# A fence between row tiles, read by two engines: sliding-window attention and a SwiGLU block on one core

## The chip, the core and the metric

The kernel runs on one core of a Trainium2 chip. A core has a matrix engine (TensorE, PE in the profile, with its weight loads on a row of their own, PEld), a vector engine (VectorE, DVE), a scalar engine (ScalarE, ACT), GpSimd (POOL) and SyncE (SP). Each engine has its own queue of instructions and works through it in order; between engines only semaphores order the work. PE writes its results to PSUM, a memory of eight banks of 128 partitions x 512 float32 values, from which DVE and ACT read them.

The metric is the time of one execution on the device in microseconds (us). Before the change it is 323.75 us, the median of 3 runs (323.66 to 324.06).

## The reference

Eight sequences of 576 tokens, 8 heads of 64 values each. Every token attends to itself and the 63 tokens before it. The result goes, as 4608 tokens of 512 values, through a SwiGLU block with 1536 hidden values:

```python
scores = (1 / sqrt(64)) * q @ k.transpose(0, 1, 3, 2)
mask = (rel >= 0) & (rel < 64)              # rel = row - column
attn = softmax(where(mask, scores, -1e9))
x = (attn @ v) laid out as 4608 x 512
g = x @ w_gate                              # 512 x 1536
out = (g * sigmoid(g) * (x @ w_val)) @ w_out    # 1536 x 512
```

## The kernel before

The 4608 tokens are worked on in nine passes of 512 tokens (t = 0 to 8). Passes 0 to 6 and 8 are the first 512 tokens of a sequence each; pass 7 (`LAST`) gathers the last 64 tokens of all eight sequences, so its scores come in 64-column pieces and there are twice as many of them. The order of the instructions is written out by hand, in Python, and each engine keeps to it. A tracking layer adds the semaphores: an instruction waits for the writers and readers of the tiles and PSUM banks that it touches.

All matmuls take bfloat16 operands. The products of the SwiGLU block use the whole 128x128 array of PE. The attention uses quarters of it: a matmul with 64 rows of operands and 64 columns of weights takes one of two **row tiles** (partitions 0 to 63 or 64 to 127 of the operands, `half(0)` and `half(1)`) and one of two column tiles (the upper or lower half of a bank). Matmuls in different quarters run at the same time.

From pass 2 on (`for t in range(1, NT)`, line 759), the attention of pass t is interleaved with the output projection of pass t-1. In the order of the code:

- `set_exp` loads ACT's table for exponentials and logarithms. `scores(t, 0)` (lines 253 to 279) writes the scores of the first four heads into the PSUM tiles `two[0]` and `two[1]`; `weigh` (line 281) makes the exponentials on ACT into `eb` (line 285), and each returned `masked()` multiplies by the mask (line 290) and adds two halves (line 295) on DVE.
- `project_quads(t - 1, tiles, range(12), 0)` (lines 464 to 475) is the first part of the output projection for token groups 0 and 2, in 64x64 quarters: row tile 0 adds up group 0 in bank 5, row tile 1 adds up group 2 in bank 7. Each covers half of the sum, over 12 blocks: 48 matmuls.
- **The fence.** The second part, `project_quads(..., 1)`, swaps the two: row tile 0 goes on with group 2 in bank 7, row tile 1 with group 0 in bank 5. A row tile may not go on in a bank while the other row tile is still writing there. So `marker(b, x)` (line 377), a 64x16 matmul of ones on row tile x into bank b, is put behind the first part on each row tile: row tile 0 into bank 4, row tile 1 into bank 6. DVE reads one value a partition from each bank into the 64x1 tile `seen` (line 768). Behind the scores of the second four heads stands one more marker, on row tile 1 into bank 6 (line 773). It overwrites what DVE reads, so it waits for DVE; and everything behind it on PE waits with it.
- Between the fence's two ends stand `masks[1]()` on DVE and `scores(t, 1)` on PE, with their exponentials on ACT and masks on DVE.
- The second part of the projection runs in two stretches (7 and 5 blocks, 28 and 20 matmuls), with `sums(t, 0, ...)` between them: PE adds up the weights (line 313) and ACT takes the logarithm (`log`, line 327). `mix_half` (line 391) multiplies weights and values, first into `two[1]`, then into `two[0]`, where the sums stood. Then come the sums of the second four heads in banks 4 and 6, the inverses (line 330), the ends of the projection (`project_end`, line 477: a copy out of PSUM by `nc.scalar.copy` or DVE, and DMAs on SP) and the remaining token groups 1 and 3 (line 459).
- `scale_all` (line 407) writes xT, and 12 calls of `gate_value` (line 446) make the gate and value products (line 450), SiLU on ACT (line 443) and their product hT on DVE (line 444), with the turning of the next pass's q and k on DVE in between (lines 208 and 218). POOL issues the loads of the pass after next once xT is there (line 791).

The short names `on_v`, `on_p` and `on_a` (line 574) are copies by DVE, POOL and ACT.

Of the kernel before, what the change touches and what calls it, by code (L numbers as in the profile page):

```python
# [9 lines left out]
FP32 = mybir.dt.float32  # L10
# [7 lines left out]
def kernel(  # L18
# [11 lines left out]
    S, D, H = 576, 64, 8  # L30
# [6 lines left out]
    cst = ctx.enter_context(tc.tile_pool(name="cst", bufs=1))  # L37
# [8 lines left out]
    bank = [two[i][:, j] for i in range(2) for j in range(2)]  # L46
# [13 lines left out]
    tri = cst.tile([P, 2, 64], BF16, name="tri")  # L60
    bias = cst.tile([P, 2, 4, 4, 2, 16], BF16, name="bias")
    seen = cst.tile([D, 1], FP32, name="seen")
    past = cst.tile([P, 1], BF16, name="past")
    mask = cst.tile([P, 8, 2, 16, 4], BF16, name="mask")

# [92 lines left out]
    def load_last_v():  # L158
        for c in range(2):
            for hd in range(H):  # L160
                w, x, h = hd // 4, hd // 2 % 2, hd % 2
                s0 = S - P + 64 * c
                nc.gpsimd.dma_start(
                    vl[64 * x:64 * x + 64, :, c, w, h],
                    v[:, hd, s0:s0 + 64].rearrange("b r d -> r b d"),
                )
# [4 lines left out]
    def stage_v(t):  # L171
        new_v(t)
        load_halves(nc.sync, staged[t, "v"], t)

    def cast_v(t):
        for i in range(4):
            js = slice(2 * i, 2 * i + 2)
            nc.gpsimd.tensor_copy(vb[t % 2][:, js], staged[t, "v"][:, js])
# [71 lines left out]
    def half(x):  # L250
        return slice(64 * x, 64 * x + 64)

    def scores(t, w):

        qT = queries[t]
        s_ps = two[0], two[1]
        for j in range(8):
            if t == LAST:
                k_j = kT[t % 2 if j < 4 else 2]
                pieces = [(j, j + 1, 0, k_j, P * (j % 4) + 64),  # L260
                          (j, j + 1, 1, k_j, P * (j % 4))]
            else:
                pieces = [(j, min(8, j + 2), 0, kT[t % 2], 64 * j)]
            for lo, hi, c, src, k0 in pieces:
                for h in range(2):
                    for x in range(2):
                        slot = s_ps[h][half(x)].rearrange("r a b -> r (a b)")
                        n = hi - lo
                        o = P * j + 64 * c
                        nc.tensor.matmul(  # L270
                            slot[:, o:o + 64 * n].rearrange(
                                "r (n e y) -> r e n y", n=n, e=16
                            ),
                            src[half(h), 2 * w + x, k0:k0 + 64],
                            blocks(qT[half(h), 2 * w + x], t, lo, hi).rearrange(
                                "r e (n y) -> r e n y", n=n
                            ),
                        )
        return [weigh(t, w, h, s_ps[h]) for h in range(2)]
# [20 lines left out]
    def ready(masks):  # L300
        for masked in masks:
            masked()
# [35 lines left out]
    def sums(t, w, tiles):  # L338
        r = room(2)
        totals(t, w, tiles if len(tiles) > 1 else [tiles[0][:, x] for x in range(2)])  # L340
        for x in range(2):
            inverse[t, 2 * w + x] = r[:, x]
        if len(tiles) > 1:
            for x in range(2):
                logs(t, r[:, x:x + 1], tiles[x].rearrange("r (b x) -> r b x", b=1))
        else:
            logs(t, r, tiles[0])
        return lambda: invert(r)
# [28 lines left out]
    def marker(b, x):  # L377
        nc.tensor.matmul(bank[b][0:D, 0:16], ones[half(x), 0:D], ones[half(x), 0:16])  # L378
# [39 lines left out]
    def mix_half(t, w, pair):  # L418
        mix(t, w, (pair[:, 0], pair[:, 1]))

    def scale_all(t, pairs):
        for u in range(4):
            scale(t, u, pairs[u // 2][:, u % 2])
# [32 lines left out]
    def project_part(t, ss, tiles, cs):  # L456
        for c in cs:
            for s, o_ps in zip(ss, tiles):
                nc.tensor.matmul(  # L459
                    o_ps[:], hT[t][:, c, P * s:P * s + P], wo[:, c, :],  # L460
                    start=(c == 0), stop=(c == 11),
                )

    def project_quads(t, tiles, cs, back):

        for c in cs:
            for y in range(2):
                for x in range(2):
                    s = 2 * (x ^ back)
                    r0 = P * s + 64 * y  # L470
                    nc.tensor.matmul(  # L471
                        tiles[s][half(y)], hT[t][half(x), c, r0:r0 + 64],
                        wo[half(x), c, :],
                        start=not back and c == 0, stop=bool(back) and c == 11,
                    )

    def project_end(t, s, o_ps, copy=nc.vector.tensor_copy):
        os_ = fsb.tile([P, 512], FP32, name="os_", tag="os_", bufs=4)
        copy(os_[:], o_ps[:])
        rows = out[S * batch(t):S * batch(t) + 512]  # L480
        if t < TURNED or t == NT - 1:
            if t < TURNED:
                rows = rows.rearrange("(r e) f -> e r f", e=4)[s]
            else:
                rows = rows[P * s:P * s + P]
            if t < TURNED or s == 0:
                for i in range(2):
                    nc.sync.dma_start(rows[half(i)], os_[half(i)])
            else:
                nc.sync.dma_start(rows, os_[:])  # L490
            return
        if t == LAST:
            rows = out.rearrange("(b s) f -> b s f", s=S)[:, 512:S]
            rows = rows.rearrange("b (r e) f -> e b r f", e=16)
        else:
            rows = rows.rearrange("(r e) f -> e r f", e=16)
        for i in range(4):
            nc.sync.dma_start(rows[4 * s + i], os_[32 * i:32 * i + 32])
# [20 lines left out]
    def set_exp():  # L519
        nc.scalar.preload_act_table_set("natural_log_exp_and_others")  # L520

    def set_silu():
        nc.scalar.preload_act_table_set("silu_and_others")
# [50 lines left out]
    on_v, on_p, on_a = nc.vector.tensor_copy, nc.gpsimd.tensor_copy, nc.scalar.copy  # L574
# [184 lines left out]
    for t in range(1, NT):  # L759
        if t > 1:  # L760
            set_exp()
            masks = scores(t, 0)
            masks[0]()
            project_quads(t - 1, tiles, range(12), 0)
            for x in range(2):
                marker(4 + 2 * x, x)
            for x in range(2):
                on_v(seen[:], bank[4 + 2 * x][0:D, 0:1])  # L768
            masks[1]()
            if t == 2:  # L770
                stage_v(3)
            ready(scores(t, 1))
            marker(6, 1)
            project_quads(t - 1, tiles, range(7), 1)
            end = sums(t, 0, two[0:1])
            project_quads(t - 1, tiles, range(7, 12), 1)
            for w in range(2):
                mix_half(t, w, two[1 - w])
            project_end(t - 1, 0, tiles[0], on_a)
            ends = end, sums(t, 1, (bank[4], bank[6]))  # L780
            for end in ends:
                end()
            project_end(t - 1, 2, tiles[2])
            project_part(t - 1, (1,), (bank[5],), range(12))
            scale_all(t, (two[1], two[0]))
            project_end(t - 1, 1, bank[5], on_a)
            project_part(t - 1, (3,), (bank[4],), range(12))
        set_silu()
        if t > 1:
            project_end(t - 1, 3, bank[4], on_v)  # L790
        on_p(past[:], xT[t][:, 3, 0:1])  # L791
        if t + 1 == LAST:
            load_last_v()
        elif t + 1 < NT and t > 1:
            cast_v(t + 1)
        if t + 2 < NT:
            load_qk(t + 2)
            if t > 1 and t + 2 != LAST:
                stage_v(t + 2)
        if t == 2:  # L800
            k_l = cast.tile([P, 4, 4, 4 * D], BF16, name="k_l", tag="c0")
        if t in (2, 3):
            load_k(k_l, [(b, S - P) for b in range(4, 8)], quarters[2 * t - 4:2 * t - 2])
        turns = (6, 7, 9, 10) if t == 1 else (1, 4, 7, 10)
        for m in range(12):
            gate_value(t, m)
            if m in turns and t + 1 < NT:
                turn(t + 1, turns.index(m))
            if (t, m) in late:
                turn_k(kT[2], k_l, late.index((t, m)))  # L810
# [32 lines left out]
```

## Time and profile before

| what | before |
| --- | --- |
| median of 3 runs | 323.75 us (323.66 to 324.06) |
| the profiled execution's own time | 324.43 us |
| its span, first to last instruction | 322.1 us |
| mean granted TensorE clock | 0.999 |
| PE busy | 314.7 us (98%) |
| DVE busy | 210.9 us (65%) |
| ACT busy | 170.0 us (53%) |
| POOL busy | 146.9 us (46%) |
| PE, line 450 (gate and value products), 814 matmuls | 211.2 us |
| PE, line 459 and line 471 (output projection) | 55.7 us and 40.0 us |
| DVE reads of the fence, line 768 | 14 of 150 ns, 2.1 us |

The profile is one execution. The span is inside the execution's own time; 2.3 us lie around it. Busy time of PE counts a matmul from its start to its modelled end, so neighbouring matmuls overlap, and their sum is not work done at full speed. The chain that ended last follows the work back from the last instruction, at each step to what released it. A row of the timeline merges neighbouring instructions of one line: its length is from the first start to the last end, and a bracket tells how long the engine stood idle before it and what ended that.

### The profile page before, as it was taken

The numbers are of one execution on the slowest core, as the hardware profiler recorded it, in microseconds if no ns is written. First come the engines' busy times: TensorE is split into PE (matmuls) and PEld (weight loads), VectorE is DVE, ScalarE is ACT, GpSimd is POOL, SyncE is SP. The second block draws the span as 40 slices with busy tenths as digits, with TensorE's granted clock in tenths as the row PEclk, the third lists the DMA queues.
The fourth block names the chain that finished last, engine by engine and source line by source line (L and its number), as shares of the span: only waits on it lengthen the run. The fifth ranks groups of instructions, "written<-read, shape, count | busy, mean of one in ns | idle before, by whom it ended". The sixth has DMA issues, their size and how long they took to land.

```text
span 322.1 us, 8061 instructions
## 1 busy us (share of the span) xinstructions
PE 314.7 (98%) x3269; PEld 155.4 (48%) x3299; DVE 210.9 (65%) x349; ACT 170.0 (53%) x232; POOL 146.9 (46%) x267
## 2 busy tenths in 40 slices
PE   8999999999999999999999999999999999999996
PEld 4644444445444544455445544454446444544443
DVE  4856756498586846776588656866896476844422
ACT  4963666348633863377336933584347633873310
POOL 4955667867567336740861099507755300000000
PEclk9999999999999999999999999999999999999999
DMA  7999999999699549983896269719998400011003
GB/s 251 202 197 198 207 155 208 201 206 125 141 192 189 57 108 167 196 93 97 146 197 70 65 117 117 76 34 144 185 192 102 101 17 1 4 72 62 0 19 113
DMA packets 83525, 40.42 MB, mean 126 GB/s; under 512 B 64160, under 2 KB 78752, under 8 KB 83488
## 3 DMA queue, kind: packets, MB, share of 16 engines
q0 software_dynamic: 51488, 22.59, 58.1%
q1 hardware_dynamic: 31456, 16.79, 23.1%
q8 instruction: 26, 0.43, 0.5%
q10 hardware_dynamic: 544, 0.52, 0.5%
q14 instruction: 11, 0.09, 0.1%
HBM read 53.02 MB, written 9.44 MB: 194 GB/s over the span
## 4 chain that ended last, share of the span: by engine, by line
PE 95%; DMA 1%; DVE 1%; issue 1%; ACT 1%; DVEq 0%
PE one L450 56%; PE one L459 17%; PE one L471 11%; PE two L391 2%; PE two L270 2%; PE one L426 2%; DMA q_f<-in_q_dram 1%; PE two L313 1%; PE one L512 1%; PE one L196 1%; DVE seen L768 1%; PE two L426 1%; PE one L378 0%; PE one L313 0%; PE two L715 0%
## 5 line engine op out<-in xcount | busy, mean ns | idle before, releaser
L443 ACT ACTIVATE sg<-one 128x512 f32<-128x512 f32 x107 | 63.9, 597 | 118.5 <-PE one L450 90.4
L444 DVE TENSOR_TENSOR hT<-sg,one 128x512 bf16<-128x512 f32 x107 | 74.0, 692 | 62.1 <-PE one L450 58.2
L450 PE MATMUL one<-xT,wv 128*128 128x512 bf16 x408 | 106.4, 379 | 0.9
L450 PE MATMUL one<-xT,wg 128*128 128x512 bf16 x406 | 104.8, 379 | 0.1
L127 POOL DMA_DIRECT2D k_s<-in_k_dram x112 | 60.5, 576 | 25.4 <-DMA q_s<-in_q_dram 12.1
L450 PEld LDWEIGHTS <-wv 128*128 128x128 bf16 x416 | 40.6, 98 | 49.2
L450 PEld LDWEIGHTS <-wg 128*128 128x128 bf16 x416 | 40.5, 98 | 48.9
L459 PE MATMUL one<-wo,hT 128*128 128x512 bf16 x241 | 55.7, 380 | 0.7 <-issue 0.2
L791 POOL COPY past<-xT 128x1 bf16<-128x1 bf16 x8 | 1.5, 190 | 92.0 <-DVE xT L407 92.0
L471 PE MATMUL one<-wo,hT 64*64 64x512 bf16 x672 | 40.0, 377 | 0.0
L459 PEld LDWEIGHTS <-hT 128*128 128x128 bf16 x252 | 23.7, 98 | 29.4 <-issue 2.0
L218 DVE STREAM_TRANSPOSE kT<-k_s 128x512 bf16<-128x512 bf16 x28 | 36.0, 1284 | 0.0
L407 DVE TENSOR_TENSOR xT<-two,r 128x512 bf16<-128x512 f32 x34 | 21.3, 684 | 22.3 <-ACT r L330 18.3
L285 ACT ACTIVATE eb<-two 128x960 bf16<-128x960 f32 (+1 forms) x32 | 29.5, 974 | 6.2 <-PE two L270 6.1
L471 PEld LDWEIGHTS <-hT 64*64 64x64 bf16 x672 | 18.4, 107 | 14.9 <-issue 1.0
L290 DVE TENSOR_TENSOR eb<-eb,mask 128x960 bf16<-128x960 bf16 (+1 forms) x32 | 21.0, 655 | 4.3 <-ACT eb L285 4.2
L208 DVE STREAM_TRANSPOSE qT<-q_s 128x512 bf16<-128x512 bf16 x32 | 22.3, 700 | 0.1
L330 ACT ACTIVATE r<-r 128x1024 f32<-128x1024 f32 (+1 forms) x20 | 18.5, 971 | 0.1
L295 DVE TENSOR_TENSOR both<-eb 128x512 bf16<-128x512 bf16 x32 | 13.6, 425 | 1.1
L92 POOL DMA_DIRECT2D q_s<-in_q_dram x24 | 13.0, 552 | 1.9 <-DMA v<-in_v_dram 1.2
L153 POOL DMA_DIRECT2D vb<-in_v_dram x16 | 10.9, 694 | 6.4 <-DMA wo<-in_moe_w_out_dram 3.7
L520 ACT ACT_TABLE_LOAD x9 | 11.5, 1283 | 2.0 <-issue 1.9
(134 smaller groups left out, 241.0 us busy)
## 6 DMA issues: line engine op xcount, KB each, us to landing
k_s<-in_k_dram POOLq DMA_DIRECT2D x112, 56.0 KB, 5.2
q_s<-in_q_dram POOLq DMA_DIRECT2D x24, 248.0 KB, 6.2
v_f<-in_v_dram SPq DMA_DIRECT2D x40, 128.0 KB
wg<-in_moe_w_gate_dram POOLq DMA_DIRECT2D x5, 256.0 KB, 8.4
wv<-in_moe_w_val_dram POOLq DMA_DIRECT2D x5, 256.0 KB, 9.0
q_f<-in_q_dram SPq DMA_DIRECT2D x4, 256.0 KB
wo<-in_moe_w_out_dram POOLq DMA_DIRECT2D x2, 512.0 KB, 10.7
vb<-in_v_dram POOLq DMA_DIRECT2D x16, 64.0 KB, 6.3
```

The lines of the kernel that those rows point to most:

```text
L127: nc.gpsimd.dma_start(k_s[p0:p0 + 32, g, :, 0:w], k[b, a:H:2, s:s + P].rearrange("u (r e) d -> r u (e d)", e=4) [:, :, 32 * c:32 * c + w],)
L208: nc.vector.transpose(queries[t][:, u, :].rearrange("r (e x) -> r e x", e=16), staged[t][0][:, u].rearrange("r (e d) -> r e d", d=D)[:, :, ...
L218: nc.vector.transpose(dst[:, u, :].rearrange("r (g x e) -> r g e x", g=4, e=4), k_s[:, :, u].rearrange("r g (e d) -> r g e d", d=D)[:, :, ...
L285: nc.scalar.activation(flat, s_ps[:].rearrange("r a b -> r (a b)")[:, 0:n], AF.Exp, scale=0.125)
L290: nc.vector.tensor_mul(flat, flat, mask[:].rearrange("r j c e y -> r (j c e y)")[:, 0:n])
L330: nc.scalar.activation(r, r, AF.Exp, scale=-1.0)
L407: nc.vector.tensor_mul(x, o_ps, r)
L443: nc.scalar.activation(sg[:], g_ps[:], AF.Silu)
L444: nc.vector.tensor_mul(hT[t][:, m, :], sg[:], v_ps[:])
L450: nc.tensor.matmul(ps[:], w[:, c, P * m:P * m + P], xT[t][:, c, :], start=(c == 0), stop=(c == 3),)
L459: nc.tensor.matmul(o_ps[:], hT[t][:, c, P * s:P * s + P], wo[:, c, :], start=(c == 0), stop=(c == 11),)
L471: nc.tensor.matmul(tiles[s][half(y)], hT[t][half(x), c, r0:r0 + 64], wo[half(x), c, :], start=not back and c == 0, stop=bool(back) and c = ...
```

## The change

The fence's two values are read by two engines. ACT reads bank 4 into a new 64x1 tile `fence`; DVE reads bank 6 into `seen`, as before. Behind the second scores there are two markers in place of one: row tile 0 into bank 4, which overwrites what ACT reads, and row tile 1 into bank 6, which overwrites what DVE reads.

```diff
     seen = cst.tile([D, 1], FP32, name="seen")
+    fence = cst.tile([D, 1], FP32, name="fence")
     past = cst.tile([P, 1], BF16, name="past")
...
             project_quads(t - 1, tiles, range(12), 0)
             for x in range(2):
                 marker(4 + 2 * x, x)
-            for x in range(2):
-                on_v(seen[:], bank[4 + 2 * x][0:D, 0:1])
+            on_a(fence[:], bank[4][0:D, 0:1])
+            on_v(seen[:], bank[6][0:D, 0:1])
             masks[1]()
             if t == 2:
                 stage_v(3)
             ready(scores(t, 1))
-            marker(6, 1)
+            for x in range(2):
+                marker(4 + 2 * x, x)
             project_quads(t - 1, tiles, range(7), 1)
```

## The prediction

> **What bounds the kernel now.** I read the profile from the outside in: the engines' busy time, the chain of work that ended last, the timeline around the fence in one token tile (the pass t=2), and the same timeline in the odd pass (t=7). Engine totals and the chain by engine:
>
> ```profile
> span 322.1 us, 8061 instructions
> PE 314.7 (98%) x3269; PEld 155.4 (48%) x3299; DVE 210.9 (65%) x349; ACT 170.0 (53%) x232; POOL 146.9 (46%) x267
> PE 95%; DMA 1%; DVE 1%; issue 1%; ACT 1%; DVEq 0%
> ```
>
> The matrix engine (PE) is busy for 98% of the span and makes up 95% of the chain. So a shorter time can only come from PE work removed or from a place where PE stands still. The other engines matter where PE waits for them. The chain of waits inside the pass t=2, in order of time, shows such a place between two groups of projection matmuls (start, length, what):
>
> ```profile
> 75.02 0.15 DVE seen L768
> 75.17 0.03 issue
> 75.19 0.02 DVEq L768
> 75.21 0.04 issue
> 75.26 0.16 DVE seen L768
> 75.42 0.04 issue
> 75.46 0.17 PE one L378
> ```
>
> The two reads by VectorE (DVE) stand one behind the other in the chain, with 0.09 us of waiting between them, and the marker behind them starts 0.04 us after the second. What the engines do meanwhile, from the timeline of the same stretch (start, length, engine, line, operation, output and input, count):
>
> ```profile
> 71.71 0.62 PE L270 MATMUL two<-qT,kT 64*64 64x128 bf16 x32
> 72.16 2.76 PE L471 MATMUL one<-wo,hT 64*64 64x512 bf16 x48
> 72.86 1.83 ACT L285 ACTIVATE eb<-two 128x960 bf16<-128x960 f32 x2
> 74.56 0.43 DVE L295 TENSOR_TENSOR both<-eb 128x512 bf16<-128x512 bf16 x1
> 74.75 0.17 PE L378 MATMUL one<-ones 64*64 64x16 bf16 x1
> 74.76 0.61 PE L270 MATMUL two<-qT,kT 64*64 64x128 bf16 x31
> 75.00 0.40 DVE L768 COPY seen<-one 64x1 f32<-64x1 f32 x2
> 75.18 0.10 PEld L378 LDWEIGHTS <-ones 64*64 64x64 bf16 x1
> 75.33 0.64 DVE L290 TENSOR_TENSOR eb<-eb,mask 128x960 bf16<-128x960 bf16 x1
> 75.41 1.83 ACT L285 ACTIVATE eb<-two 128x960 bf16<-128x960 f32 x2 [0.72 <-PE two L270]
> 75.46 0.17 PE L378 MATMUL one<-ones 64*64 64x16 bf16 x1
> 75.46 1.22 PEld L471 LDWEIGHTS <-hT 64*64 64x64 bf16 x28 [0.18 <-issue]
> 75.47 1.71 PE L471 MATMUL one<-wo,hT 64*64 64x512 bf16 x28
> ```
>
> The scores of the second head group (L270) cover part of the fence: they end at 74.76+0.61 = 75.37. The ends of matmuls are latencies, though. Without a fence, the first scores end at 71.71+0.62 = 72.33 and the projection starts at 72.16, 0.17 earlier. So the second projection could start at 75.37-0.17 = 75.20, and it starts at 75.47: the fence costs 0.27 us here.
>
> The pass t=7 has twice as many, shorter score matmuls:
>
> ```profile
> 240.49 0.71 PE L270 MATMUL two<-qT,kT 64*64 64x64 bf16 x64
> 241.02 2.77 PE L471 MATMUL one<-wo,hT 64*64 64x512 bf16 x48
> 241.64 1.94 ACT L285 ACTIVATE eb<-two 128x1024 bf16<-128x1024 f32 x2
> 243.61 0.18 PE L378 MATMUL one<-ones 64*64 64x16 bf16 x2
> 243.62 0.77 PE L270 MATMUL two<-qT,kT 64*64 64x64 bf16 x64
> 243.87 0.40 DVE L768 COPY seen<-one 64x1 f32<-64x1 f32 x2
> 244.33 0.17 PE L378 MATMUL one<-ones 64*64 64x16 bf16 x1
> ```
>
> The same arithmetic gives an earliest restart of 243.62+0.77-0.18 = 244.21, with 0.18 = 240.49+0.71-241.02. The restart is at 244.33, so 0.12 us is lost. The fence is in seven passes, t=2 to 8, and the count of its reads says so:
>
> ```profile
> L768 DVE COPY seen<-one x14: 149/150/151, 75.0 to 278.4; 64x1 f32<-64x1 f32 x14
> ```
>
> All fourteen take 149 to 151 ns, so I take six passes like t=2 and one like t=7.
>
> **The change part by part.** Prices for ScalarE (ACT), by shape, and one ACT copy in the same table set:
>
> ```profile
> L285 ACT ACTIVATE eb<-two 128x960 bf16<-128x960 f32 x28 | 25.6, 968 | 5.3 <-PE two L270 5.3
> L285 ACT ACTIVATE eb<-two 128x1024 bf16<-128x1024 f32 x4 | 3.9, 1020 | 0.9 <-PE two L270 0.9
> 78.54 0.59 ACT L479 COPY os__1314<-one 128x512 f32<-128x512 f32 x1
> ```
>
> *One DVE read becomes an ACT read.* No row has a small ACT operation. The two exponentials give (1020-968)/64 = 0.81 ns per element and 968-960x0.81 = 190 ns for none, so a 64x1 copy is put at 0.19 us, an estimate. It cannot sensibly be under the 0.15 us of the DVE read; the upper end is the 128x512 copy, 0.59 us. I take 0.19 because the exponentials, which read the same memory, differ from the copy in length alone. Hops between engines: PE to ACT 0.05 and ACT to PE 0.05, from these rows:
>
> ```profile
> 77.00 0.39 PE L313 MATMUL two<-both,ones 64*64 64x512 bf16 x4
> 77.44 1.02 ACT L327 ACTIVATE r<-two 128x1024 f32<-128x1024 f32 x1 [0.20 <-PE two L313]
> 4.24 0.63 ACT qk_b L577
> 4.92 1.03 PE one L196 x8
> ```
>
> (77.00+0.39 = 77.39 against 77.44; 4.24+0.63 = 4.87 against 4.92.) The first markers end at 74.75+0.17 = 74.92. The ACT read then runs from 74.97 to 75.16 and releases PE at 75.21. ACT is free for it: the exponentials ahead of it end at 72.86+1.83 = 74.69, and in t=7 at 243.58 against markers at 243.79. Behind it on ACT stands the next exponential, which starts at 75.41 when the scores end, 0.25 us after the read is through; if that cover were gone, every us of ACT lateness would be paid by the exponentials.
>
> *The remaining DVE read* starts at 75.00 (its own queue is free at 74.56+0.43 = 74.99) and ends at 75.15; with the 0.04 to 0.06 us from the second read to the marker now, it releases PE at 75.21 too. The DVE work behind it, the mask product at 75.33, moves up by the read and the wait that go, about 0.26 us. PE does not wait for it.
>
> *The own tile for each reader* costs memory of four bytes a row and no instruction. *The second marker* adds one weight load and one 64x16 matmul in each of seven passes. The first markers start within 0.01 us of each other, and the projection's first matmul starts 0.01 us after the marker that waited. So I take 0.02 us a pass. From above, the whole weight load of 0.10 us (L378 at 75.18) could be exposed.
>
> *DMA, POOL and SP:* nothing is added, removed or moved past another; their work starts as much earlier as PE does.
>
> *Sum.* In t=2: released at the latest of 75.21 (ACT), 75.21 (DVE) and 75.20 (PE itself), plus 0.02 for the second marker and the 0.01 that stands today: 75.24 against 75.47, so 0.23 us. Six such passes: 1.38. In t=7 ACT would release at 243.79+0.05+0.19+0.05 = 244.08 and DVE at 243.87+0.15+0.06 = 244.08, both before PE's own 244.21; with the 0.02, 244.23 against 244.33: 0.10. Together 1.5 us. The profiled execution took 324.43 us (its span of 322.1 and 2.3 around it); it becomes 322.9. The median of the runs is 323.75, 0.7 below the profiled one, and becomes **322.3 us**, 0.45% less. A difference of 0.2%, or 0.65 us, is about what measurement can tell.
>
> *A rule on the second marker's weight load.* The row first: the projection's weight load starts at 75.46, with the marker that waited, after 0.18 us in which the loader had nothing issued; so it did not pass the waiting marker. The Trainium skill (TensorE: Matmul & The Clock Gate, The mechanism) says that a weight load for another row group is pulled ahead of matmuls in flight. By that rule the second marker's load, in the other row half, would be hidden and the second marker free, 0.14 us better in all; by the row, it is not pulled past a wait, and up to 0.10 us a pass is exposed. The row decides here, and gives the first rival below.
>
> **The rivals.** *The second marker pays its weight load.* Behind a marker of row tile 0 that still waits stands the load for row tile 1. If it is not hidden, a pass like t=2 loses 0.10 instead of 0.02: 6x0.08 = 0.5 less gain. In t=7 ACT releases 0.13 before PE is done, so it hides. That gives 322.8. For it: the 0.18 us of "issue". Against it: today's projection stands in the same position, and its first matmul is only 0.01 after the marker.
>
> *The gain is given back later in the pass.* The scores stay where they are, so the exponentials do too; only PE behind the fence moves up. Next in line:
>
> ```profile
> 78.30 1.01 PE L391 MATMUL two<-eb,vb 64*64 64x128 bf16 x64
> ```
>
> Its second half writes what the logarithm (L327) reads. That half starts near 78.30+0.4 = 78.70; the logarithm ends at 77.44+1.02 = 78.46. With PE 0.23 earlier the logarithm no longer waits for L313 (77.39 becomes 77.16) but for the exponentials' end at 75.41+1.83 = 77.24; it ends at about 78.30 and is wanted at 78.47. Of 0.24 us slack, 0.17 stay. If I have misplaced a wait by more than that, up to all of the gain goes: 323.75.
>
> *Slower: the ACT read comes late.* The new release decides against the old one when 74.97 + read + 0.05 + 0.02 passes 75.46, at a read of 0.42 us. At 0.59, the upper end, PE restarts 0.17 us later than now in a pass like t=2, and in t=7 at 243.84+0.59+0.05+0.02 = 244.50, 0.17 later too: 7x0.17 = 1.2, so 324.95 us. The DVE reads at 0.15 speak against it, as a read of the same size in the same memory.
>
> *A table load for the copy.* If the copy were not in the loaded set, two loads would stand around each read, 1.28 us each:
>
> ```profile
> L520 ACT ACT_TABLE_LOAD x9 | 11.5, 1283 | 2.0 <-issue 1.9
> ```
>
> Each fence would then release over 1 us later, 7 us and more in all: above 330. Against it: nine loads are one for each of nine token tiles, and the copy at 78.54 runs between a logarithm and the next without one. The Trainium skill (ScalarE: Activation LUTs, Table sets: the hidden batching unit) says that cheap functions such as copy are in every set; the trace agrees.
>
> **How the numbers follow.** Forecast 0.60 (322.3), weight load paid 0.18 (322.8), given back 0.10 (323.75), ACT late 0.11 (324.95), table load 0.01. The first two are faster by over 0.65 us; a few hundredths of the second may fall short of it. So faster 0.76, same 0.12, slower 0.12. The low end is no fence cost at all: 6x0.27+0.12 = 1.7, 322.0, and a little for scatter, 321.9. The high end takes in "given back", 323.8, and leaves out the late read.
>
> **What would show it.** Right: one DVE read of 0.15 us and one ACT read near 0.19 us that start within 0.05 us of each other; the second markers about 0.46 us after the start of the first ones; the projection's second part starting about 0.49 us after them (75.24-74.75) instead of 0.72; no other wait that grows in the seven passes; PE's span 1.5 us shorter with the same busy time. Wrong: an ACT read over 0.4 us, a gap between the second markers near 0.1 us, a wait of L391 for ACT, or a table load beyond nine.

## The result and the profile after

The changed kernel takes 322.15 us (median of 4 runs, 321.89 to 322.59) against 323.9 us of the kernel before (4 runs): a ratio of 0.9946, with a 95% interval of 0.9929 to 0.9963. Measured again later beside 15 runs of the kernel before, it is 0.9929 (0.9916 to 0.9941), 1.9 to 2.7 us less. The forecast was 322.3 us.

The profiled execution of the changed kernel took 321.89 us. Because of the added lines, line 450 is now 451, 471 is 472, and so on; the two reads are lines 768 (ACT) and 769 (DVE). The engine totals and the chain by engine:

```profile
span 319.9 us, 8068 instructions
PE 312.8 (98%) x3276; PEld 154.9 (48%) x3306; DVE 210.1 (66%) x342; ACT 170.9 (53%) x239; POOL 147.0 (46%) x267
PE 96%; DMA 1%; issue 1%; DVE 1%; ACT 1%; DVEq 0%
```

Seven PE instructions more (the second markers), seven DVE instructions fewer and seven more on ACT: that is the edit. The chain of waits in the pass t=2:

```profile
73.98 0.43 PE one L472 x8
74.41 0.46 PE two L271 x30
74.86 0.04 PE one L379 x2
74.90 1.10 PE one L472 x15
```

DVE is gone from it. Where two reads and the waits between them stood, the chain goes from the projection through the scores into the second markers without leaving PE. The chain goes by the modelled ends of matmuls, though: that the fence still costs something is shown below, by the kernel without one. The timeline of the same stretch (start, length, engine, line, operation, output and input, count):

```profile
71.65 2.76 PE L472 MATMUL one<-wo,hT 64*64 64x512 bf16 x48
74.24 0.17 PE L379 MATMUL one<-ones 64*64 64x16 bf16 x1
74.25 0.62 PE L271 MATMUL two<-qT,kT 64*64 64x128 bf16 x31
74.49 0.15 ACT L768 COPY fence<-one 64x1 f32<-64x1 f32 x1 [0.31 <-PE one L379]
74.53 0.15 DVE L769 COPY seen<-one 64x1 f32<-64x1 f32 x1
74.60 0.64 DVE L291 TENSOR_TENSOR eb<-eb,mask 128x960 bf16<-128x960 bf16 x1
74.70 0.20 PE L379 MATMUL one<-ones 64*64 64x16 bf16 x2
74.74 1.27 PE L472 MATMUL one<-wo,hT 64*64 64x512 bf16 x20
74.91 1.83 ACT L286 ACTIVATE eb<-two 128x960 bf16<-128x960 f32 x2 [0.26 <-PE two L271]
```

Both reads take 0.15 us and lie side by side, 0.04 us apart. The second markers go off from 74.70 on, the one into bank 6 at 74.73 (74.70+0.20-0.17), 0.05 us after the DVE read has ended; the projection's second part starts at 74.74. From the first matmul of the first part it is now 74.74-71.65 = 3.09 us, where it was 75.47-72.16 = 3.31 before: 0.22 us less. The pass t=7:

```profile
239.44 2.78 PE L472 MATMUL one<-wo,hT 64*64 64x512 bf16 x48
242.05 0.78 PE L271 MATMUL two<-qT,kT 64*64 64x64 bf16 x64
242.63 0.19 PE L379 MATMUL one<-ones 64*64 64x16 bf16 x2
242.65 1.71 PE L472 MATMUL one<-wo,hT 64*64 64x512 bf16 x28
```

3.21 us here, against 244.33-241.02 = 3.31 before: 0.10 less. I call this time "part 1 to part 2" below. The other stretch, "part 2 to the next part 1", is 30.44 to 30.57 us from t=2 to t=6 in both kernels, so what the fence gives is not taken back by another wait. Behind t=7 it is shorter too, by 0.25 us, which nothing in the change asks for: 275.34-244.33 = 31.01 before, and 30.76 after.

### The profile page after: what moved, and what is told of

Read it like the earlier page. It is cut to its first block, busy times and chain, and to the rows that moved or that the text cites. A ratio compares the mean times of both kernels' runs of the same rounds, so it can differ in the third digit from the quotient of the medians.

```text
span 319.9 us, 8068 instructions
## 1 busy us (share of the span) xinstructions
PE 312.8 (98%) x3276; PEld 154.9 (48%) x3306; DVE 210.1 (66%) x342; ACT 170.9 (53%) x239; POOL 147.0 (46%) x267
## 4 chain that ended last, share of the span: by engine, by line
PE 96%; DMA 1%; issue 1%; DVE 1%; ACT 1%; DVEq 0%
PE one L451 56%; PE one L460 17%; PE one L472 11%; PE two L271 3%; PE two L392 2%; PE one L427 2%; DMA q_f<-in_q_dram 1%; PE two L314 1%; PE one L513 1%; PE two L427 1%; PE one L314 0%; PE one L197 0%; DVE kT L200 0%; PE two L242 0%; PE two L716 0%
```

## The experiments

All times of the table are differences of starts of projection matmuls (lines 471 or 472) in one profile of each kernel; the values of part 1 to part 2 are those of t=2 to 6 and 8, which agree within 0.02 us but for one.

| kernel | part 1 to part 2 | in t=7 | part 2 of t=7 to part 1 of t=8 | first part 1 at | ratio to before (95%) |
| --- | --- | --- | --- | --- | --- |
| before | 3.31 | 3.31 | 31.01 | 72.16 | 1 |
| before, second profile | 3.31 | 3.32 | 31.04 | 71.66 | - |
| before, third profile | 3.31 | 3.31 | 31.25 | 71.66 | - |
| the change | 3.09 | 3.21 | 30.76 | 71.65 | 0.9946 (0.9929 to 0.9963) |
| the change, second profile | 3.09 | 3.21 | 30.76 | 71.64 | 0.9929 (0.9916 to 0.9941) |
| own tiles, both on DVE | 3.12 | 3.19 | 31.35 | 71.89 | 0.9965 (0.9953 to 0.9977) |
| the same with two markers | 3.12 | 3.21 | 30.76 | 71.89 | 0.9952 (0.9939 to 0.9965) |
| own tiles, both on ACT | 3.12 | 3.19 | 30.91 | 72.44 | 0.9963 (0.9949 to 0.9977) |
| before with two markers | 3.31 | 3.31 | 30.79 | 71.65 | 0.9998 (0.9987 to 1.0009) |
| long read on ACT | 3.33 | 3.34 | 30.77 | 72.44 | 0.9994 (0.9984 to 1.0004) |
| no fence | 3.02 | 3.27 | 31.25 | 71.91 | 0.9939 (0.9921 to 0.9956) |
| before, six matmuls more at the start | 3.31 | 3.31 | 30.76 | 71.57 | 0.9989 (0.9977 to 1.0001) |

**Own tiles, both reads on DVE.** The theory was that a second engine gives the gain. Its rival: it is the wait between two writes of one tile.

```diff
-            on_a(fence[:], bank[4][0:D, 0:1])
+            on_v(fence[:], bank[4][0:D, 0:1])
             on_v(seen[:], bank[6][0:D, 0:1])
...
-            for x in range(2):
-                marker(4 + 2 * x, x)
+            marker(6, 1)
             project_quads(t - 1, tiles, range(7), 1)
```

> Both values are read by VectorE, as before, but each into its own tile, and the one marker stays. I look at the time from the first matmul of the projection's first part to the first of its second part: 3.31 us before (72.16 to 75.47 in the pass t=2), 3.09 after the change (71.65 to 74.74). If the gain comes from a second engine, the two reads of 0.15 us still stand in series: they end 0.30 us after the first starts, and the time is 3.20, half of the gain (0.11 x 6 passes and 0.09 in t=7: 0.75 us). If it comes from the wait between two writes of the same tile, the second read can follow the first as closely as the mask product follows a read now (0.07 us, 75.26 to 75.33): reads through 0.22 us after the first starts, the time is 3.12, and nearly all of the gain comes without ScalarE (0.19 x 6 and 0.10: 1.2 us).

Measured: 3.12 us, the number of the rival. The timeline of this kernel, in t=2:

```profile
74.74 0.15 DVE L768 COPY fence<-one 64x1 f32<-64x1 f32 x1
74.82 0.14 DVE L769 COPY seen<-one 64x1 f32<-64x1 f32 x1
75.01 0.17 PE L379 MATMUL one<-ones 64*64 64x16 bf16 x1
75.02 0.63 PE L472 MATMUL one<-wo,hT 64*64 64x512 bf16 x8
```

The reads start 0.08 us apart and overlap; before, they started at 75.00 and 75.26, about 0.25 apart. The row of the kernel before that names the difference is a separate semaphore instruction in DVE's queue (DVEq) at the reads' line, one for each pass:

```profile
L768 DVEq EVENT_SEMAPHORE  x7: 21/21/21, 75.2 to 278.4; - x7
```

The trace has it wait on the very counter that the first read raises at its end; in t=2 it goes off at 75.19, after that end at 75.15. With two tiles it is gone from that line. So the second read waited until the first had written `seen`, and that wait was 0.19 of the 0.22 us. The whole kernel gains less (0.9965) than six times 0.19 and 0.12 make, 1.26 us or 0.9961, by an amount that the interval does not tell apart from nothing; its profile also shows a longer standstill behind t=7, to which I come below.

**Both reads on ACT**, each into its own tile, one marker:

```diff
             on_a(fence[:], bank[4][0:D, 0:1])
-            on_v(seen[:], bank[6][0:D, 0:1])
+            on_a(seen[:], bank[6][0:D, 0:1])
...
-            for x in range(2):
-                marker(4 + 2 * x, x)
+            marker(6, 1)
```

> ScalarE reads both values, each into its own tile, and one marker waits. If what counts is that the reads need not wait for each other, the second read follows the first within about 0.1 us, as on VectorE with own tiles, and the parts stand 3.10 to 3.16 us apart. If two reads on ScalarE stand in full series (0.15 and 0.15), it is 3.20. If ScalarE cannot do without the second engine at all, it is 3.3 as before.

Measured: 3.12 us. Two reads on one engine overlap here too (timeline, t=2):

```profile
75.29 0.15 ACT L768 COPY fence<-one 64x1 f32<-64x1 f32 x1 [0.31 <-PE one L379]
75.35 0.15 ACT L769 COPY seen<-one 64x1 f32<-64x1 f32 x1
75.55 0.17 PE L379 MATMUL one<-ones 64*64 64x16 bf16 x1
```

They start 0.06 us apart. (ACT's queue has a semaphore instruction between them too, but it waits on DVE's counter, not on the first read, and goes off at 75.29 while that read runs.) Either engine does alone what the two do together, to 0.03 us, as long as the reads have a tile each.

**Own tiles and two markers**, so that only the second engine is missing from the change:

```diff
-            on_a(fence[:], bank[4][0:D, 0:1])
+            on_v(fence[:], bank[4][0:D, 0:1])
             on_v(seen[:], bank[6][0:D, 0:1])
```

> Both reads by VectorE into a tile of their own, and the second marker on both row tiles, so that only the second engine is missing from the change. With own tiles and one marker the parts stood 3.12 us apart, against 3.09 after the change and 3.31 before. Expected here: 3.12 to 3.14 in six passes, so 0.2 to 0.3 us over the changed kernel in all. If the standstill in t=7 (0.44 us with own tiles and one marker) hangs on the place of PE's instructions, it is gone here, and the time is within 0.3 us of the changed kernel's; if ScalarE has to do with it, it stays.

Measured: 3.12 us, and the stretch behind t=7 is 30.76 as in the changed kernel. Against the change its profile lacks 6 x 0.03 = 0.2 us at the fence and starts its first projection 0.25 us later. By the ratios it is slower than the change by 0.0006 (0.2 us) if the change's first measurement is taken, and by 0.0023 (0.7 us), with intervals that touch, if the second is; so the second engine is worth 0.2 us by the profile, and somewhere from there to 0.7 by the runs.

**The second marker alone**, on the kernel before:

```diff
-            marker(6, 1)
+            for x in range(2):
+                marker(4 + 2 * x, x)
             project_quads(t - 1, tiles, range(7), 1)
```

> The kernel before with the second marker alone: both reads by VectorE into one tile. If the second marker costs little, as I put it, the time between the projection's parts grows from 3.31 to 3.33 us, 0.15 us in all, which the runs do not tell from nothing. If its weight load is paid, it grows to 3.41, 0.7 us in all. In the pass t=7 the values' matmuls stood still for 0.12 us before the change and not after it; if that hangs on the place of PE's instructions alone, it is gone here too, since PE has as many as after the change.

Measured: 3.31 us and a ratio of 0.9998; the second marker costs nothing here. Its timeline in t=2 says why:

```profile
74.49 0.41 DVE L768 COPY seen<-one 64x1 f32<-64x1 f32 x2
74.70 0.42 PE L378 MATMUL one<-ones 64*64 64x16 bf16 x2
74.95 0.62 PE L471 MATMUL one<-wo,hT 64*64 64x512 bf16 x6
```

The pair of markers starts at 74.70, when the first read is through, and the projection at 74.95: the marker into bank 4 goes off while the one into bank 6 still waits. After the change the pair's start and the projection's are 0.04 us apart, against 0.01 with one marker, but that is not the marker's price either: the marker into bank 6 waits for the DVE read, which ends 0.03 to 0.04 us after the ACT read. Own tiles with one marker and with two both give 3.12 us; only in t=7 do they differ, 3.19 against 3.21. So the weight load of 0.10 us is hidden.

**A longer read on ACT**, 320 values a partition in place of one:

```diff
-    fence = cst.tile([D, 1], FP32, name="fence")
+    fence = cst.tile([D, 320], FP32, name="fence")
...
-            on_a(fence[:], bank[4][0:D, 0:1])
+            on_a(fence[:], bank[4][0:D, 0:320])
```

> The changed kernel with a longer read on ScalarE: 320 values a partition of bank 4 in place of one; the values are not used. At 0.153 us for one and 0.81 ns for each more the read takes 0.41 us. If PE's restart is set by the later of the two reads, it comes 0.24 us later than after the change: 3.33 us between the projection's parts in all seven passes, and the time is that of before to within 0.2 us, the gain gone. If ScalarE's read is off the path, the time between the parts stays at 3.09 and so does the gain.

Measured: 3.33 us, and 0.9994 of the time before: the gain is gone, and the time between the parts is the expected one. The timeline in t=2:

```profile
75.29 0.42 ACT L768 COPY fence<-one 64x320 f32<-64x320 f32 x1 [0.31 <-PE one L379]
75.33 0.15 DVE L769 COPY seen<-one 64x1 f32<-64x1 f32 x1
75.76 0.20 PE L379 MATMUL one<-ones 64*64 64x16 bf16 x2
75.78 0.64 PE L472 MATMUL one<-wo,hT 64*64 64x512 bf16 x8
```

The DVE read is over at 75.48; PE goes on 0.05 us after the ACT read has ended at 75.71. So PE waits for the later of the two, and a read of 0.42 us brings back the time before, which is where the prediction put the point from which the change is a loss.

**No fence**, an edit of the kernel before. The row tiles are not swapped, so none is needed; this kernel leaves out one half of the sums of token groups 0 and 2 and adds the other half twice:

```diff
-                    s = 2 * (x ^ back)
+                    s = 2 * x
...
-            for x in range(2):
-                marker(4 + 2 * x, x)
-            for x in range(2):
-                on_v(seen[:], bank[4 + 2 * x][0:D, 0:1])
...
-            marker(6, 1)
             project_quads(t - 1, tiles, range(7), 1)
```

> No fence at all: no markers and no reads, and the row tiles are not swapped in the second part, so that none is needed. This adds the first half of the sums of token groups 0 and 2 twice and leaves their second half out; the number and the shape of the matmuls are the same. By my sum the time between the parts falls to 3.04 us (PE's own restart), 0.05 under the changed kernel in each pass, and the whole is 1.7 us under before and 0.3 under the change. If the second half of the projection is held by something else than the fence, it stays near 3.09; if the fence costs PE more than the profile's model of its ends says, it falls clearly under 3.04.

Measured: 3.02 us in six passes, 0.02 under my figure.

```profile
74.50 0.61 PE L270 MATMUL two<-qT,kT 64*64 64x128 bf16 x32
74.92 0.61 PE L471 MATMUL one<-wo,hT 64*64 64x512 bf16 x8
```

The second part starts 0.19 us before the scores' modelled end here; I had taken 0.17. The fence costs 0.29 us a pass before, and 0.07 after the change. The whole is no faster than the changed kernel (0.9939 against 0.9929 to 0.9946): the 6 x 0.07 = 0.4 us go against 0.49 us behind t=7 and 0.06 in it. The pass t=7 does not measure the fence here. Its scores take 0.87 us instead of the 0.77 of before, because PE pauses within them:

```profile
241.84 0.87 PE L270 MATMUL two<-qT,kT 64*64 64x64 bf16 x64
```

**The standstill behind t=7.** PE pauses within the values' matmuls (line 391 or 392) of t=7, in some kernels. The timelines of the kernel before, of own tiles on DVE, and of the third profile of the kernel before:

```profile
247.63 0.99 PEld L391 LDWEIGHTS <-v 64*64 64x64 bf16 x105 [0.23 <-issue]
```

```profile
245.81 0.39 PE L392 MATMUL two<-eb,v 64*64 64x64 bf16 x23
246.64 1.10 PE L392 MATMUL two<-eb,v 64*64 64x64 bf16 x105 [0.44 <-issue]
```

```profile
246.65 0.35 PE L391 MATMUL two<-eb,v 64*64 64x64 bf16 x23
247.36 1.10 PE L391 MATMUL two<-eb,v 64*64 64x64 bf16 x105 [0.35 <-issue]
```

It comes after 23 of the 128 matmuls. Without a fence PE has three matmuls fewer in each of six passes by then, 18 in all, and there it comes after 41: the same place in PE's program, with 2655 weight loads before it in all six traces that have the pause (the expectation below calls it number 5312). With two markers that place comes after 17 of the 128 matmuls, and there is no pause. To tell the place from the fence I left the fence as before and added six small matmuls at the very start:

```diff
     keep_warm(6)
+    for _ in range(6):
+        nc.tensor.matmul(warm[0:D, 0:16], ones[:, 0:D], ones[:, 0:16])
     nc.gpsimd.memset(tri[:], 1.0)
```

> The kernel before with six more small warming matmuls at the very start, while PE still waits for the first data; the fence is untouched. In t=7 every PE instruction then has the same place in PE's program as in the changed kernel. In the three kernels without a second marker PE stood still in the values' matmuls of t=7 (0.12, 0.44 and 0.34 us) at the same place of its program, the instruction with the number 5312; in the three with it, it did not. If the place alone decides, the standstill is gone here, and the stretch from the projection's second part in t=7 to its first part in t=8 is 30.8 us, against 31.0 before; between the parts it stays 3.31. If the standstill goes with the fence's shape, it is there.

Measured: 30.76 us, and the matmuls run through, as in the changed kernel:

```profile
246.71 1.32 PE L391 MATMUL two<-eb,v 64*64 64x64 bf16 x128
```

```profile
245.48 1.33 PE L392 MATMUL two<-eb,v 64*64 64x64 bf16 x128
```

(The first row is of the kernel with the six matmuls, the second of the changed kernel.) All six profiles in which the instructions have the changed kernel's place give 30.76 to 30.79 us; all six in which they have the place of before, or the one of no fence, give 30.91 to 31.35. So the 0.15 to 0.59 us go with the place, not with the fence: the changed kernel is rid of the pause because it has one more matmul a pass.

What PE waits for there was not tried by a run, and the timeline says only that nothing was issued. The DMA transfers in the traces point to the fetching of instructions (row of the kernel before: queue, kind, transfers, MB, share of the DMA engines' time):

```profile
q8 instruction: 26, 0.43, 0.5%
```

These are 26 transfers of 16 KiB for PE's 3299 weight loads, one for every 127 of them. In the six profiles with the pause, the last such transfer ahead of it ends 0.9 to 1.3 us before PE comes to the place, and PE goes on 1.4 to 1.6 us after that end. In the six without, PE comes to the place 2.5 us or more after it. The pause in the scores of t=7 without a fence fits this: it lies 128 weight loads earlier in the program, and PE goes on 1.5 us after a transfer's end.

One pass (t=2) of the kernel with the six matmuls took 3.45 us from part 1 to part 2, and that is another matter. DVE was behind with its queue there: it began its reads 3.00 us after the start of part 1 (74.57-71.57), against 2.84 before (75.00-72.16), and PE waited for them. Whether the six matmuls have to do with it, one profile can't tell.

**Two more profiles of the kernel before**, for what was left of the difference:

> The kernel before once more, for a second profile. The fence's seven passes and the stretch behind t=7 explain 1.4 and 0.25 us of a gain that the closest ratio puts at 1.9 to 2.7. The profile of before also came 0.5 us later to its first fence (72.16 us against 71.65 and 71.64 after the change). If that belongs to the kernel before, the first projection starts near 72.16 again; if it is scatter of the first loads and of the instruction supply at the start, it lies anywhere between 71.6 and 72.4, as in the other kernels, whose code up to there hardly differs. The parts stand 3.31 us apart in all passes, and t=7 has its standstill of 0.1 us or more.

> The same, a third profile: the first projection anywhere from 71.6 to 72.4 us if the start scatters, near 72.16 if it is the kernel's; 3.31 us between the parts; a standstill in t=7.

Measured: both came to their first projection at 71.66 us, like the changed kernel, and their spans are 321.6 and 321.8 us. So the 0.5 us by which the first profile of before was later is scatter of the start; other kernels with the same code up to there lie between 71.64 and 72.44. Against these two, the changed kernel's span of 319.9 is 1.7 and 1.9 us shorter, and the parts add up: 6 x 0.22 + 0.10 = 1.42 at the fence, 0.28 and 0.49 behind t=7. That lies within the interval of the first ratio (1.2 to 2.3 us) and at the lower edge of the second's (1.9 to 2.7); what goes beyond 1.9 us lies outside the span. In the second measurement the median fell by 2.16 us (323.9 to 321.74), and the median span of the same runs by 1.8 (321.7 to 319.9). A run of the three kernels that read twice into one tile (before, two markers, six matmuls more) takes 2.14 to 2.42 us longer than its span, a run of any other kernel here 1.74 to 2.05. Why is open.

The changed kernel stayed the fastest that keeps the computation; nothing in the experiments pointed to a version that beats it by more than the 0.07 us a pass that its fence still costs.

## Why the prediction was right, and where it was not

- **What bounds the kernel, and the price of the fence.** Right: PE stands still at the fence. I put its whole cost at 0.27 us in a pass like t=2 and 0.12 in t=7; without the fence it is 0.29 in the former (3.31-3.02). The 0.12 was not tested: without the fence t=7 is only 0.04 us shorter, with PE's pause in its scores.
- **The sum.** 0.23 us in each of six passes and 0.10 in t=7, 1.48 in all, against 0.22 and 0.10, 1.42 measured. Counted from the start of part 1, I put the three releases at 3.05 us (ACT), 3.05 (DVE) and 3.04 (PE itself). ACT's came so (74.70-71.65). DVE's came 0.04 later, because its read started 0.11 us after the first markers' end and not 0.08 as before; PE itself would have been ready at 3.02. The 0.03 put on top for the markers made up for it. One sign was not sharp: the same busy time of PE was forecast, and it is 313.8 to 314.7 us in the profiles before and 312.8 and 313.2 after.
- **The ACT read.** Put at 0.19 us from the slope of two exponentials; it took 0.153. It started 0.08 us after the markers' end rather than 0.05, so the release came out the same. The line through two long operations overstates a short one by a quarter.
- **The own tile.** This is the step that failed. "The own tile for each reader costs memory of four bytes a row and no instruction": I booked it at nothing and gave the whole gain to the second engine. The runs show the reverse. Own tiles alone, on one engine, give 0.19 of the 0.22 us; the second engine adds 0.03. I had the sign of it in view, the 0.09 us between the reads in the chain, and did not ask what the second read waited for. So the total came out right with the gain on the wrong part: tile and engine were changed at once, and the total does not speak for the mechanism that I gave.
- **The second marker.** 0.02 us a pass forecast. Own tiles with one marker and with two show nothing in six passes (3.12 both) and 0.01 in t=7; added to the kernel before, it costs nothing either. The rival with a paid weight load (322.8 us) is out.
- **Given back later.** It is not: part 2 to the next part 1 is unchanged in five passes, to 0.04 us.
- **Late ACT read, table load.** Neither: 0.153 us, and as many table loads as before, nine at the line that I counted (520, now 521) and nine more in `set_silu` (523, now 524), which I did not count. The point from which a late read loses was put at 0.42 us, and the read of 0.42 us did come out even with before.
- **Not foreseen.** 0.25 to 0.49 us behind t=7, from the place of PE's instructions, and some 0.4 us outside the span, where I left the 2.3 us of before as they were. So it is in part chance that the first median, 322.15, lies beside the forecast of 322.3: the second, 321.74, is below the low end of 321.9.

## What to carry to other kernels

Before giving a short job to a second engine, look at what the second of two short operations waits for: two writes of one scratch tile are put in order by a wait, and a tile for each frees the same engine to overlap them. Where two things change together (a tile, an engine), do each alone; the total was forecast well here with the gain on the wrong part. And this kernel's time moved by up to 0.6 us with where PE's instructions lie, so compare the stretch that was changed, pass by pass, beside the total.

## What the runs showed of the hardware

- Two 64x1 reads of PSUM on DVE start 0.08 us apart with a tile each, and 0.25 us apart into one tile, with a semaphore instruction between them. The Trainium skill (VectorE: DVE Perf Modes, The DRAIN you can't avoid) says that a semaphore after each operation costs nothing extra in a chain of copies. Here, with short operations and the later one waiting for the earlier, the wait costs about 0.18 us.
- A 64x1 copy on ACT takes 0.153 us, a 64x320 copy 0.418: 0.83 ns for each further value, and the same as DVE (0.15) for one value. The Trainium skill (ScalarE: Activation LUTs, What ACT_TABLE_LOAD costs) gives 186 ns and 0.833 ns a value for an ACTIVATE with immediate scale and bias. For the copy here the slope agrees, and the fixed part is 34 ns less (152).
- PE lost 0.15 to 0.59 us at one place of its program (30.91 to 31.35 us against 30.76), in a stretch of 128 short matmuls, and nothing when the place moved by six matmuls. It went on 1.4 to 1.6 us after the end of a 16 KiB instruction transfer; that it waited for this transfer is read from the traces, not shown by a run.
